# Sparse attention with a gated feed-forward: the softmax transposed by blocks on VectorE, the values product written straight into the columns of x

## The chip, the cores and the metric

The kernel runs on one core of one Trainium2 chip. The metric is the device time of one execution in microseconds (us), the median over runs; smaller is better. A core has TensorE (PE, matmuls, and beside it PEld, its weight loads), VectorE (DVE), ScalarE (ACT), GpSimd (POOL) and SyncE (SP), which issues the transfers here. Matmul results land in PSUM, eight banks of 128 partitions by 512 fp32 columns.

## The reference

Attention over 8 batches, 8 heads, 576 positions and 64 dimensions, then a feed-forward layer over its 4608 tokens (dm 512, dff 2048):

```python
scores = scale * np.matmul(q, k.transpose(0, 1, 3, 2))
mask_local = (rel >= 0) & (rel < 32)
mask_strided = (rel >= 0) & (pos[None, :] % 32 == pos[:, None] % 32)
...
attn = softmax(where(mask, scores, -1e9)) ; o = matmul(attn, v)
x = o.transpose(0, 2, 1, 3).reshape(B * S, H * D)
h = x @ w_in ; g = h * sigmoid(h) ; out = g @ w_out
```

Heads 0 to 3 use the local mask: a position sees itself and the 31 before it. Heads 4 to 7 use the strided one: a position sees the earlier ones with the same remainder by 32, at most 18. Everything is fp32.

## The kernel before, in words

**Tiles of the attention.** The host gathers q and k (`kqt`, dimensions on partitions, two heads on the 128 partitions) and v (`vt`) so that only the small blocks the masks leave are computed. A batch has six groups; the order in a batch is local, strided, local, strided, local, strided. A local group has 12 tiles of 32 queries by 64 keys for two heads, and a strided group 8, 8 or 6 tiles of 54 queries (3 remainders times 18) padded to 64 rows. Scores of a group stand in two PSUM banks (one for each head) as n column blocks of 128 rows: n is 3 for a local group (four tiles on top of one another in a block) and 4, 4 or 3 for the strided ones (two tiles in a block). `self.tiles` fixes which tile lies in which row block and column block, and so the order in which the matmuls are issued: before, tile t goes to column block `t // per` and row block `t % per`, so neighbouring tiles lie in different row blocks.

**Stages of a group** (methods of `Attention`). `scores` (L384) multiplies q and k, two matmuls a tile. `peak` (L402, and the exponential of ScalarE at L408) masks, takes the maximum and the exponential into `sm`, with the sums. `total` (L428, L429) makes reciprocals of the sums; `scale` (L432) multiplies `sm` by them, for strided groups alone. `turn` (L438) transposes `sm` on TensorE, one 128x128 matmul with the identity a column block, into a bank; `turned` (L442) copies that to `pt`. `values` multiplies by v: for a local group (L455) with rows of queries as the output, which `share` (L471) normalises into `xq` and `back` (L491) transposes on TensorE again, and `done` (L496) copies into `xb`; for a strided group (L460) with the head's dimensions as rows, which `sorted` (L484) copies into `xb` in the order of the positions. `xb` holds a batch's x, transposed, in fp32.

**Feed-forward.** The 4608 tokens are nine blocks of 512, and dff is 16 chunks of 128. For a block and chunk, `hidden` (L525) runs 12 matmuls of 128x128 by 128x512 over dm into one bank; `tanh` (L535, ScalarE), `gate` (L539), `ghi` (L547) and `glo` (L551, all VectorE) make the gated value and split it into a rounded part and a rest; `output` (L571) adds 12 more matmuls into four banks `po` that live through the block. fp32 precision comes from three products of rounded parts (hi by hi, hi by lo, lo by hi). At a block's end `store` copies each `po` on ScalarE into `osb` (L579), of which there are two, and sends it out. x is split into xhi and xlo at L513 and L517.

**Order.** PSUM is a ring `ps` of four banks, taken in turn by score halves, transposes, values and hidden chunks, and the four `po`. The first two batches, the loading of weights and block 0 are placed by a planner (`Steps`, `attention_steps`): each step has a cost on one or two engines and a due time, and it is put where it can start first; gaps on TensorE before 60 us are filled with transposes of the identity (L639). From block 1 on the order is written by hand: a chunk's `hidden`, its gating, and the `output` of the chunk before. At the chunks 0, 3, 5, 8, 11 and 13 of a block `between` inserts one **step** of the next batch's attention, behind the output:

```python
            c = plan[k, fc]
            turn(c + 1)
            back(c - 1)
            values(c)
            scores(c + 2)
            total(c + 2)
```

Of the kernel before, what the change touches and what calls it, by code (L numbers as in the profile page):

```python
# [28 lines left out]
P = 128  # L29
# [11 lines left out]


KW = 64
SEQ = 3 * NJ
QW = 448
VT = 12
KBUFS = 2
VBUFS = 2
KFIRST = 4
VFIRST = 6  # L50
XBUFS = NP + 2
# [6 lines left out]
class Group:  # L58
    def __init__(self, local, first, count):
        self.local, self.first, self.count = local, first, count  # L60
        self.rows = STRIDE if local else KW
        self.per = P // self.rows
        self.n = count // self.per
        step = STRIDE if local else SEQ
        self.q0 = [step * t for t in range(count)]
        half = S // STRIDE
        gap = [STRIDE if local and first < half <= first + t else 0 for t in range(count)]
        self.k0 = [q0 + g for q0, g in zip(self.q0, gap)]
        self.nq = self.q0[-1] + self.rows
        self.nk = self.k0[-1] + KW  # L70

        self.starts = [
            tuple(t % self.per for t in range(c * self.per, (c + 1) * self.per)
                  if local and (first + t) % half == 0)
            for c in range(self.n)
        ]
# [117 lines left out]
def sparse_attention_ffn(ctx: ExitStack, tc: tile.TileContext, kqt, vt, w_in, w_out, out):  # L194
# [55 lines left out]
    m = mask("mask_strided")  # L250
    for t in range(P // KW):
        keep(m, t * KW, KW, [4, NJ], [-NJ, -1], 0, 1)
        keep(m, t * KW, KW, [4, NJ], [NJ, 0], NJ - 1, -1)
    masks[False, ()] = m
# [98 lines left out]
    class Attention:  # L353


        def __init__(self, b, at):
# [83 lines left out]
        def turned(self, engine="ACT"):  # L440
            self.pt = att.tile([P, 512], F32, name="pt")
            copy[engine](out=self.pt[:, : self.cols], in_=self.psp[:, : self.cols])  # L442

        def values(self):
# [5 lines left out]
            for t, c, rows in self.tiles:  # L450
                p0 = c * P + rows.start
                for h in range(2):
                    at = slice(h * KW, (h + 1) * KW)
                    if g.local:
                        nc.tensor.matmul(  # L455
                            self.pso[h][rows, c * D : (c + 1) * D],
                            pt[at, p0 : p0 + g.rows], vbd[at, t], start=True, stop=True,
                        )
                    else:
                        nc.tensor.matmul(  # L460
                            self.pso[h * D : (h + 1) * D, t * SEQ : (t + 1) * SEQ], vbd[at, t],
                            pt[at, p0 : p0 + SEQ], start=True, stop=True,
                        )

        def share(self):
# [7 lines left out]
        def sorted(self):  # L473
            g, pso = self.g, self.pso

            places = STRIDE + 1
            at, end = 3 * g.first, 3 * (g.first + g.count)
            while at < end:
                hp, r = divmod(at, places)
                n = min(end - at, STRIDE - r)  # L480
                s0 = at - 3 * g.first
                src = pso[:, s0 * NJ : (s0 + n) * NJ].rearrange("p (r j) -> p r j", j=NJ)
# [10 lines left out]
        def done(self, engine="ACT"):  # L493
            flat = place_of(self.b).rearrange("p n s -> p (n s)")
            x0 = self.g.first * STRIDE
            copy[engine](out=flat[:, x0 : x0 + self.cols], in_=self.psx[:, : self.cols])  # L496

# [93 lines left out]
    def attention_steps(c, due, last=None):  # L591
# [16 lines left out]
        soft = e  # L608
        if not local:
            soft = add(f"N{c}", {"DVE": 0.14 + 0.14 * n}, t1 - 1, [r], a.scale)  # L610
        if last == "S":
# [4 lines left out]
                lambda: a.turned(p.engine), takes=["pt"], gives=[t])  # L616
        if last == "T":
            return
        v = add(f"v{c}", {"SP": P * a.g.count * D * 4 / RATE}, t2 - 5, [],
# [111 lines left out]
    nexts = [attention_steps(NG + i, burst[i : i + 4]) for i in range(NG)]  # L731
    attention_steps(2 * NG, (late[0], late[1], 0, 0), "T")
    attention_steps(2 * NG + 1, (late[1], late[1] + 8, 0, 0), "S")
# [24 lines left out]


    def scores(c):  # L760
        if c < len(groups):
# [11 lines left out]
    def turn(c):  # L773
        if c < len(groups):
            groups[c].turn()
            groups[c].turned()

    def values(c):
        if c < len(groups):
# [5 lines left out]
    def back(c):  # L785
        if groups[c].g.local:
            groups[c].back()
            groups[c].done()

# [99 lines left out]
```

## Time and profile before

| | us |
|---|---|
| median of 3 runs (920.74 to 921.81) | 921.0 |
| the profiled execution | 923.33 |
| its span | 921.5 |
| TensorE busy | 904.5 (98%) |
| VectorE busy | 436.6 (47%) |
| ScalarE busy | 315.1 (34%) |
| share of the chain that ended last: PE, DVE, DMA, ACT | 87%, 7%, 3%, 2% |

The span goes from the first to the last instruction of the profiled execution. The chain that ended last is followed back from the last instruction to what released each one. The largest groups are the matmuls of the hidden chunks (L525) and of the output (L571), 39% of that chain each.

### The profile page before, as it was taken

How to read it: one execution, taken by the hardware profiler on the slowest of the kernel's cores; microseconds unless marked ns; L12 is line 12 of the kernel's file. 1: busy time of each engine (PE TensorE's matmuls, PEld its weight loads, DVE VectorE, ACT ScalarE, POOL GpSimd, SP SyncE). 2: the span in 40 equal slices, each digit the busy share in tenths (PEclk: the TensorE clock that was granted, in tenths of full speed). 3: DMA queues.
4: the chain of work that ended last, by engine and by line, in shares of the span. 5: the costliest groups of instructions: out<-in, count | busy, mean ns of one | idle time of the engine just before them, and what ended most of it. 6: DMA issues, size and time to landing. Idle time of an engine off the chain costs nothing.

```text
span 921.5 us, 18028 instructions
## 1 busy us (share of the span) xinstructions
PE 904.5 (98%) x7451; PEld 742.9 (81%) x7451; DVE 436.6 (47%) x1408; ACT 315.1 (34%) x897; POOL 19.0 (2%) x38
## 2 busy tenths in 40 slices
PE   8999998999999999999999999999999999999997
PEld 6777776888888888888888888888888888888886
DVE  6999665434534444434444353444443333333332
ACT  3877453422532243224342252234332221112112
POOL 4100000000000000000000000000000000000000
PEclk9999999999999999999999999999999999999999
DMA  9674533201301102112220131120210010001001
GB/s 336 217 244 155 161 101 102 64 29 38 114 27 41 63 32 91 54 29 69 83 63 30 39 101 40 37 66 32 87 40 9 1 46 1 1 1 46 1 1 46
DMA packets 34962, 63.04 MB, mean 68 GB/s; under 512 B 2624, under 2 KB 22080, under 8 KB 34880
## 3 DMA queue, kind: packets, MB, share of 16 engines
q1 hardware_dynamic: 34880, 61.89, 20.3%
q8 instruction: 58, 0.95, 0.4%
q14 instruction: 24, 0.20, 0.1%
HBM read 52.45 MB, written 9.44 MB: 67 GB/s over the span
## 4 chain that ended last, share of the span: by engine, by line
PE 87%; DVE 7%; DMA 3%; ACT 2%; issue 0%; ACTq 0%; SPq 0%
PE ps L525 39%; PE po L571 39%; PE ps L384 3%; PE ps L460 2%; DMA stage<-w_in 2%; PE ps L438 1%; PE ps L455 1%; DVE stage L287 1%; DVE w L327 1%; DVE glo L551 1%; DVE sm L402 1%; PE ps L491 1%; DMA stage<-w_out 1%; DVE th L539 1%; PE ps L639 1%; ACT stage L276 1%
## 5 line engine op out<-in xcount | busy, mean ns | idle before, releaser
L525 PE MATMUL ps<-xhi,w 128*128 128x512 f32 x1152 | 386.6, 395 | 2.2 <-DVE th L539 1.5
L525 PEld LDWEIGHTS ps<-xhi,w 128*128 128x128 f32 x1152 | 216.2, 188 | 50.5 <-DVE th L539 1.9
L539 DVE SCALAR_TENSOR_TENSOR th<-th,ps 128x512 f32<-128x512 f32 (+1 forms) x147 | 99.3, 675 | 319.2 <-ACT th L535 319.1
L535 ACT ACTIVATE th<-ps 128x512 f32<-128x512 f32 (+1 forms) x147 | 86.3, 587 | 430.0 <-PE ps L525 427.7
L525 PE MATMUL ps<-xlo,w 128*128 128x512 f32 x576 | 225.2, 391 | 1.7 <-DVE xlo L517 1.7
L571 PE MATMUL po<-w,ghi 128*128 128x512 f32 x504 | 155.4, 390 | 0.7 <-ACT ghi L547 0.7
L525 PEld LDWEIGHTS ps<-xlo,w 128*128 128x128 f32 x576 | 108.2, 188 | 23.8 <-DVE xlo L517 3.0
L571 PEld LDWEIGHTS po<-w,ghi 128*128 128x128 f32 x504 | 94.4, 188 | 20.4 <-ACT ghi L547 0.8
L551 DVE TENSOR_TENSOR glo<-th,ghi 128x512 fp32r<-128x512 f32 (+1 forms) x147 | 100.3, 682 | 12.2 <-ACT ghi L547 1.6
L571 PE MATMUL po<-w,glo 128*128 128x512 f32 x252 | 98.3, 390 | 0.3 <-DVE glo L551 0.3
L571 PE MATMUL po<-stage,ghi 128*128 128x512 f32 x288 | 88.7, 389 | 0.0
L408 ACT ACTIVATE sm<-sm,sums 128x64 f32<-128x64 f32 x226 | 75.5, 336 | 13.2 <-DVE sums L402 12.6
L571 PE MATMUL po<-v,ghi 128*128 128x512 f32 x216 | 66.7, 390 | 0.0
L571 PEld LDWEIGHTS po<-stage,ghi 128*128 128x128 f32 x288 | 54.1, 188 | 11.3
L547 DVE CAST ghi<-th 128x512 fp32r<-128x512 f32 (+1 forms) x137 | 57.7, 421 | 10.4
L571 PEld LDWEIGHTS po<-w,glo 128*128 128x128 f32 x252 | 47.3, 188 | 11.0 <-DVE glo L551 1.2
L571 PE MATMUL po<-stage,glo 128*128 128x512 f32 x144 | 56.1, 389 | 0.0
L442 ACT COPY pt<-ps 128x384 f32<-128x384 f32 (+1 forms) x40 | 20.6, 514 | 79.8 <-PE ps L438 79.8
L571 PEld LDWEIGHTS po<-v,ghi 128*128 128x128 f32 x216 | 40.4, 188 | 8.5 <-ACT ghi L547 0.2
L571 PE MATMUL po<-k,ghi 128*128 128x512 f32 x144 | 44.3, 389 | 0.0
L571 PE MATMUL po<-v,glo 128*128 128x512 f32 x108 | 42.2, 391 | 0.4 <-DVE glo L551 0.4
L408 ACT ACTIVATION_READ_ACCUMULATOR sm<-sm,sums 128x1 f32 x226 | 42.6, 188 | 0.0
(77 smaller groups left out, 737.1 us busy)
## 6 DMA issues: line engine op xcount, KB each, us to landing
v<-vt SPq DMA_DIRECT2D x24, 384.0 KB, 3.6
out<-osb SPq DMA_DIRECT2D x36, 256.0 KB, 2.0
stage<-w_in SPq DMA_DIRECT2D x16, 512.0 KB, 4.8
stage<-w_out SPq DMA_DIRECT2D x16, 512.0 KB, 3.6
k<-kqt SPq DMA_DIRECT2D x16, 442.0 KB, 4.0
k<-kqt SPq DMA_DIRECT2D x16, 416.0 KB, 4.6
v<-vt SPq DMA_DIRECT2D x16, 256.0 KB, 2.8
k<-kqt SPq DMA_DIRECT2D x8, 448.0 KB, 4.2
```

Source lines behind the costliest of these rows:

```text
L276: nc.scalar.activation(out=value, in_=value, func=AF.Prelu, scale=2.0**-112, alpha=-(2.0**32))
L287: nc.vector.scalar_tensor_tensor(out=upper, in0=upper, scalar=3, in1=lower, op0=ALU.logical_shift_left, op1=ALU.bitwise_or,)
L384: nc.tensor.matmul(self.pss[h][rows, c * KW : (c + 1) * KW], kbd[at, 1, g.q0[t] : g.q0[t] + g.rows], kbd[at, 0, g.k0[t] : g.k0[t] + KW], s ...
L408: nc.scalar.activation(out=s_sb[:, c, h], in_=s_sb[:, c, h], func=AF.Exp, bias=peaks[:, c, h : h + 1], scale=-1.0, accum_out=rsum[:, c, h ...
L442: copy[engine](out=self.pt[:, : self.cols], in_=self.psp[:, : self.cols])
L460: nc.tensor.matmul(self.pso[h * D : (h + 1) * D, t * SEQ : (t + 1) * SEQ], vbd[at, t], pt[at, p0 : p0 + SEQ], start=True, stop=True,)
L525: nc.tensor.matmul(ph, weight(0, wi, fc)[:, cc * P : (cc + 1) * P], x[xi][cc], start=(cc, n) == (0, 0), stop=(cc, n) == (NP - 1, 2),)
L535: nc.scalar.activation(out=th[:, cols], in_=ph[:, cols], func=AF.Tanh, scale=0.5)
L539: nc.vector.scalar_tensor_tensor(out=th[:, cols], in0=th[:, cols], scalar=1.0, in1=ph[:, cols], op0=ALU.add, op1=ALU.mult,)
L547: copy[engine](out=g[0][:, cols], in_=th[:, cols])
L551: nc.vector.tensor_sub(out=g[1][:, cols], in0=th[:, cols], in1=g[0][:, cols].bitcast(F32))
L571: nc.tensor.matmul(po[tt], g[gi][:, cols], weight(1, wi, fc), start=fc == 0 and n == 0, stop=fc == NFC - 1 and n == 2,)
```

## The change

From the third batch on, all of the following. `scale` is applied to local groups as well. `turn_by_blocks` replaces `turn` and `turned`: VectorE transposes `sm` in blocks of 32x32 into `pt`, with two instructions over 128 partitions (each block stays on its own 32 partitions) and four over 32 partitions (the block goes to the neighbouring 32). `values_by_halves` replaces `values`, `share` and `back`: v is the stationary side for both kinds, the head's dimensions are the output's rows and the positions its columns; one half of a group's tiles reads the partitions 0 to 63, the other half 64 to 127, each half into a bank of its own, and `done_by_halves` copies them into `xb` on ScalarE. All of it but the values runs at the step that makes the scores, so `between` holds `values(c)` and `scores(c + 2)` alone.

For all batches, the first two included: `Group.at` numbers tiles down the column blocks of a row block first (tile t in column block `t % n`, row block `t // n`), so `self.tiles` issues all tiles of a row block before the next row block. Strided queries are padded to 64 in the host's layout (`QW` 448 to 512), and each group of 54 is cut in two halves of 27 at columns 0 and 32. Batches 0 and 1 keep the transposes on TensorE. In the planner the scale step is added for the group 2 * NG, and its transpose falls away: two `turn_by_blocks` stand ahead of block 1 instead.

```diff
+        self.at = [(t % self.n, t // self.n) for t in range(count)]
...
             self.tiles = [
-                (t, t // g.per, slice(t % g.per * g.rows, (t % g.per + 1) * g.rows))
-                for t in range(g.count)
+                (t, c, slice(r * g.rows, (r + 1) * g.rows)) for t, (c, r) in enumerate(g.at)
             ]
...
+        def turn_by_blocks(self):
+            n, size = self.g.n, P // STRIDE
+            pt = att.tile([P, 512], F32, name="pt")[:, : self.cols]
+            self.pt = pt = pt.rearrange("k (s c h q) -> k s c h q", s=2, h=2, q=STRIDE)
+            src = self.sm[:, : self.cols].rearrange("p (c h s k) -> p s c h k", h=2, s=2, k=STRIDE)
+            for s in range(2):
+                nc.vector.transpose(out=pt[:, s], in_=src[:, s])
+            for r in range(size):
+                rows, to = (slice(i * STRIDE, (i + 1) * STRIDE) for i in (r, r ^ 1))
+                nc.vector.transpose(out=pt[to, r % 2], in_=src[rows, 1 - r % 2])
...
+        def values_by_halves(self):
+            g, pt, vbd = self.g, self.pt, self.vbd
+            self.pso = [self.bank("pso") for _ in range(2)]
+            half, size = g.count // 2, STRIDE if g.local else SEQ
+            for i in range(half):
+                for p in range(2):
+                    c, r = g.at[p * half + i]
+                    at = slice(p * KW, (p + 1) * KW)
+                    for h in range(2):
+                        moved = pt[at, r % 2, c, h] if g.local else pt[at, :, c, h, :HALF]
+                        nc.tensor.matmul(
+                            self.pso[p][h * D : (h + 1) * D, i * size : (i + 1) * size],
+                            vbd[at, 2 * i + h], moved, start=True, stop=True,
+                        )
+
+        def done_by_halves(self):
+            g = self.g
+            half = g.count // 2
+            if g.local:
+                flat = place_of(self.b).rearrange("p n s -> p (n s)")
+                for p in range(2):
+                    x0, n = (g.first + p * half) * STRIDE, half * STRIDE
+                    nc.scalar.copy(out=flat[:, x0 : x0 + n], in_=self.pso[p][:, :n])
+                return
+            for p in range(2):
+                first = g.first + p * half
+                self.sort(self.pso[p], 3 * first, 3 * (first + half))
...
     def scores(c):
         if c < len(groups):
             groups[c].scores()
             scored.add(c)
             load_due()
             groups[c].peak()
-
-    def total(c):
-        if c < len(groups):
             groups[c].total()
-            if not groups[c].g.local:
-                groups[c].scale()
...
+            groups[c].scale()
+            groups[c].turn_by_blocks()
 
     def values(c):
-        if c < len(groups):
-            groups[c].values()
-            weighed.add(c)
-            load_due()
-            (groups[c].share if groups[c].g.local else groups[c].sorted)()
...
+        groups[c].values_by_halves()
+        weighed.add(c)
+        load_due()
+        groups[c].done_by_halves()
...
         if (k, fc) in plan:
-            c = plan[k, fc]
-            turn(c + 1)
-            back(c - 1)
-            values(c)
-            scores(c + 2)
-            total(c + 2)
-
+            values(plan[k, fc])
+            scores(plan[k, fc] + 2)
+
+    for c in (2 * NG, 2 * NG + 1):
+        groups[c].turn_by_blocks()
```

Line numbers shift: in the changed kernel the scores are at L389, the exponential at L413, the values at L495, hidden at L580, tanh at L590, gate at L594, ghi at L602, glo at L606, output at L626, the idle transposes at L692.

TensorE's order at a block's first step (a local group; `stage` names hold w_out), before:

```order
L571 MATMUL po<-stage_1734,ghi 128x512
L571 MATMUL po<-stage_1730,glo 128x512
L438 MATMUL ps<-ident,sm 128x128 x4
L455 MATMUL ps<-v_77,pt 32x64 x24
L384 MATMUL ps<-k_80 32x64 x24
L525 MATMUL ps<-xhi,w_0_616 128x512
```

and of the changed kernel:

```order
L626 MATMUL po<-stage_1769,ghi 128x512
L626 MATMUL po<-stage_1767,glo 128x512
L495 MATMUL ps<-pt,v_77 64x32 x24
L389 MATMUL ps<-k_80 32x64 x24
L580 MATMUL ps<-xhi,w_0_598 128x512
```

The four transposes of the next group are gone; 24 values and 24 scores stand between the output and the hidden chunk as before, the values with 32 moving columns instead of 64 and 64 output rows instead of 32.

TensorE at the second step (a strided group), before:

```order
L571 MATMUL po<-w_0_701,glo 128x512
L438 MATMUL ps<-ident,sm 128x128 x3
L491 MATMUL ps<-ident,xq 128x128 x3
L460 MATMUL ps<-pt,v_77 64x54 x16
L384 MATMUL ps<-k_81 64x64 x16
L525 MATMUL ps<-xhi,w_0_616 128x512
```

and now:

```order
L626 MATMUL po<-w_0_709,glo 128x512
L495 MATMUL ps<-pt,v_77 64x54 x16
L389 MATMUL ps<-k_81 64x64 x16
L580 MATMUL ps<-xhi,w_0_598 128x512
L580 MATMUL ps<-xlo,w_0_598 128x512
```

Both sets of transposes are gone, the next group's softmax and the result of the local group before.

VectorE behind the scores of a strided group with n = 4, before:

```order
L428 TENSOR_SCALAR sums<-sums 128x8
L429 RECIPROCAL sums<-sums 128x8
L432 TENSOR_TENSOR sm<-sm,sums 128x512
L539 SCALAR_TENSOR_TENSOR th<-th,ps 128x512
L547 CAST ghi<-th 128x512
L551 TENSOR_TENSOR glo<-th,ghi 128x512
```

and now:

```order
L433 TENSOR_SCALAR sums<-sums 128x8
L434 RECIPROCAL sums<-sums 128x8
L437 TENSOR_TENSOR sm<-sm,sums 128x512
L594 SCALAR_TENSOR_TENSOR th<-th,ps 128x512
L459 STREAM_TRANSPOSE pt<-sm 128x256 x2
L602 CAST ghi<-th 128x512
L462 STREAM_TRANSPOSE pt<-sm 32x256 x4
L606 TENSOR_TENSOR glo<-th,ghi 128x512
```

The six block transposes stand between the gate and glo of the hidden chunk of that step.

## Rows read from the trace of the kernel before

**Rows 1.** Windows by stage: us, busy by engine, PEclk, DMA, GB/s.

```profile
0.00:113.00 113.00, 104.63 (x1294) 82.94 (x1294) 93.41 (x321) 70.14 (x125) 17.04 (x36) 0.98 0.67 222
148.40:728.30 579.90, 579.90 (x5010) 479.93 (x5007) 252.29 (x892) 195.92 (x682) 0.00 (x0) 1.00 0.16 52
```

**Rows 2.** Timeline of PE at a local step: start, us, line, tiles, count.

```profile
446.38 0.60 PE L438 MATMUL ps<-ident,sm 128*128 128x128 f32 x4
446.91 0.72 PE L455 MATMUL ps<-v,pt 64*32 64x64 f32 x48
447.43 0.93 PE L384 MATMUL ps<-k 64*32 64x64 f32 x48
448.29 0.50 PE L525 MATMUL ps<-xhi,w 128*128 128x512 f32 x1
```

**Rows 3.** Timeline of PE at the next step, a strided one.

```profile
464.74 0.49 PE L438 MATMUL ps<-ident,sm 128*128 128x128 f32 x3
...
465.49 1.07 PE L460 MATMUL ps<-pt,v 64*64 64x54 f32 x29
466.35 0.27 PE L384 MATMUL ps<-k 64*64 64x64 f32 x1
466.35 0.22 PE L460 MATMUL ps<-pt,v 64*64 64x54 f32 x1
...
466.40 0.23 PE L460 MATMUL ps<-pt,v 64*64 64x54 f32 x2
...
467.03 0.50 PE L525 MATMUL ps<-xhi,w 128*128 128x512 f32 x1
```

**Rows 4.** Timeline of PE, last step of the same batch, first and last row.

```profile
527.81 0.49 PE L438 MATMUL ps<-ident,sm 128*128 128x128 f32 x3
...
529.87 0.50 PE L525 MATMUL ps<-xhi,w 128*128 128x512 f32 x1
```

**Rows 5.** Timeline of PE in the first 40 us: strided scores, local scores.

```profile
13.02 0.69 PE L384 MATMUL ps<-k 64*64 64x64 f32 x32
13.64 0.72 PE L455 MATMUL po<-v,pt 64*32 64x64 f32 x48
...
28.15 0.72 PE L384 MATMUL ps<-k 64*32 64x64 f32 x48
28.80 0.44 PE L639 MATMUL ps<-ident 128*128 128x128 f32 x2
```

**Rows 6.** Timeline of ACT at two block starts, 444 and 743 us.

```profile
444.53 1.28 ACT L579 ACTIVATE osb<-po 128x512 f32<-128x512 f32 x2
...
742.95 1.28 ACT L579 ACTIVATE osb<-po 128x512 f32<-128x512 f32 x2
745.67 1.29 ACT L579 ACTIVATE osb<-po 128x512 f32<-128x512 f32 x2 [1.45 <-DMA out<-osb]
```

**Rows 7.** Lines by form: line, tiles, count, busy us, mean ns, idle before.

```profile
L547 DVE CAST ghi<-th 128x512 fp32r<-128x512 f32 x133 | 56.8, 427 | 10.3
L484 ACT COPY xb<-ps 128x144 f32<-128x144 f32 x7 | 2.9, 408 | 2.3 <-PE ps L460 2.3
L517 DVE TENSOR_TENSOR xlo<-xb,xhi 128x256 fp32r<-128x256 f32 x8 | 3.1, 422 | 4.2 <-ACT xhi L513 4.2
L517 DVE TENSOR_TENSOR xlo<-xb,xhi 128x192 fp32r<-128x192 f32 x8 | 2.8, 354 | 4.0 <-ACT xhi L513 4.0
```

**Rows 8.** Timeline of DVE at a step with n = 4.

```profile
533.51 0.69 DVE L432 TENSOR_TENSOR sm<-sm,sums 128x512 f32<-128x512 f32 x1
534.12 0.68 DVE L539 SCALAR_TENSOR_TENSOR th<-th,ps 128x512 f32<-128x512 f32 x1
```

**Rows 9.** Critical chain in order of time: start, us, what.

```profile
443.81 2.72 PE po L571 x12
...
448.36 2.94 PE ps L525 x12
```

**Rows 10.** Timeline of PE where block 1 begins.

```profile
146.44 0.63 PE L438 MATMUL ps<-ident,sm 128*128 128x128 f32 x4 [1.84 <-DVE sm L432]
```

More of the change, by code (lines that the diff above doesn't have):

```diff
@@ L49 @@
 KFIRST = 4
+EARLY = 2
 VFIRST = 6
@@ L63, in __init__ @@
         self.n = count // self.per
-        step = STRIDE if local else SEQ
-        self.q0 = [step * t for t in range(count)]
+        self.q0 = [self.rows * t for t in range(count)]
         half = S // STRIDE
         gap = [STRIDE if local and first < half <= first + t else 0 for t in range(count)]
-        self.k0 = [q0 + g for q0, g in zip(self.q0, gap)]
+        self.k0 = [(STRIDE if local else SEQ) * t + g for t, g in enumerate(gap)]
         self.nq = self.q0[-1] + self.rows
         self.nk = self.k0[-1] + KW
+        self.at = [(t % self.n, t // self.n) for t in range(count)]
         self.starts = [
-            tuple(t % self.per for t in range(c * self.per, (c + 1) * self.per)
-                  if local and (first + t) % half == 0)
+            tuple(r for t, (at, r) in enumerate(self.at)
+                  if at == c and local and (first + t) % half == 0)
             for c in range(self.n)
@@ L250, in sparse_attention_ffn @@
     m = mask("mask_strided")
-    for t in range(P // KW):
-        keep(m, t * KW, KW, [4, NJ], [-NJ, -1], 0, 1)
-        keep(m, t * KW, KW, [4, NJ], [NJ, 0], NJ - 1, -1)
+    for t in range(P // STRIDE):
+        q0 = t % 2 * HALF
+        keep(m, t * STRIDE, STRIDE, [4, NJ], [-NJ, -1], q0, 1)
+        keep(m, t * STRIDE, STRIDE, [4, NJ], [NJ, 0], NJ - 1 - q0, -1)
     masks[False, ()] = m
@@ L440, in turned @@
         def turned(self, engine="ACT"):
-            self.pt = att.tile([P, 512], F32, name="pt")
-            copy[engine](out=self.pt[:, : self.cols], in_=self.psp[:, : self.cols])
+            pt = att.tile([P, 512], F32, name="pt")
+            copy[engine](out=pt[:, : self.cols], in_=self.psp[:, : self.cols])
+            self.pt = pt[:, : self.cols].rearrange("k (c r q) -> k c r q", r=P // STRIDE, q=STRIDE)
+        def turn_by_blocks(self):
[8 more added lines that the diff above has]
+                nc.vector.transpose(out=pt[to, r % 2], in_=src[rows, 1 - r % 2])
         def values(self):
@@ L450, in values @@
             for t, c, rows in self.tiles:
-                p0 = c * P + rows.start
+                r = rows.start // STRIDE
                 for h in range(2):
@@ L456, in values @@
                             self.pso[h][rows, c * D : (c + 1) * D],
-                            pt[at, p0 : p0 + g.rows], vbd[at, t], start=True, stop=True,
+                            pt[at, c, r], vbd[at, t], start=True, stop=True,
                         )
@@ L473, in sorted, with sort @@
         def sorted(self):
-            g, pso = self.g, self.pso
+            g = self.g
+            self.sort(self.pso, 3 * g.first, 3 * (g.first + g.count))
+        def sort(self, pso, first, end):
             places = STRIDE + 1
-            at, end = 3 * g.first, 3 * (g.first + g.count)
+            at = first
             while at < end:
@@ L495, in done @@
             x0 = self.g.first * STRIDE
[L496 removed]
+            dst = flat[:, x0 : x0 + self.cols].rearrange(
+                "p (r c q) -> p c r q", c=self.g.n, q=STRIDE
+            )
+            src = self.psx[:, : self.cols].rearrange("p (c r q) -> p c r q", c=self.g.n, q=STRIDE)
+            copy[engine](out=dst, in_=src)
     def new_x():
@@ L608, in attention_steps @@
         soft = e
-        if not local:
+        if not local or a.b >= EARLY:
             soft = add(f"N{c}", {"DVE": 0.14 + 0.14 * n}, t1 - 1, [r], a.scale)
@@ L865, in rows @@
         flat = np.concatenate([flat, np.zeros((B, 2, 1, D), a.dtype)], axis=2)
-        tiles = flat[:, :, where].transpose(0, 2, 1, 4, 3, 5)
-        return np.ascontiguousarray(tiles).reshape(B, NG, P, VT, D)
+        tiles = flat[:, :, where]
+        by_head = tiles[:EARLY].transpose(0, 2, 1, 4, 3, 5).reshape(EARLY, NG, P, VT, D)
+        by_tile = np.zeros((B - EARLY, NG, 2, KW, VT // 2, 2, D), a.dtype)
+        for gi, g in enumerate(GROUPS):
+            half = g.count // 2
+            some = tiles[EARLY:, :, gi, : g.count].reshape(B - EARLY, 2, 2, half, KW, D)
+            by_tile[:, gi, :, :, :half] = some.transpose(0, 2, 4, 3, 1, 5)
+        return np.concatenate([by_head, by_tile.reshape(B - EARLY, NG, P, VT, D)])
     kq = np.ascontiguousarray(np.stack([columns(k, k_from), columns(q, q_from)], axis=3))
```

22 lines of the change are left out of this document (7 added, 15 removed).

## The prediction

> **What bounds the kernel now.** Read the stages first [rows 1]. Up to 113 us TensorE is busy 104.6 us, with VectorE at 93.4 of 113 beside it; from 148.4 to 728.3 us TensorE is busy for every microsecond while VectorE is at 252 of 580 and ScalarE at 196. So from 148 us on only TensorE's own instructions, or a new wait on it, move the end. This stage holds the attention of the batches 2 to 7, which is what the change rewrites. Next, TensorE by itself in such a stretch, at a local step [rows 2] and at a strided step [rows 3]. A step is all that stands between an output and the next hidden chunk: 446.38 to 448.29 (1.91 us) and 464.74 to 467.03 (2.29 us). Read in the same way, the six steps of a batch take 1.91, 2.29, 1.91, 2.17, 1.70 and 2.06 us, in all 12.04; the last of them is in [rows 4].
>
> Three prices come from these rows. A 128 by 128 transpose costs 0.11 us: six of them and the change to small tiles behind them take 464.74 to 465.49, 0.75 us, so 0.10 is the change of shape. A matmul with 64 rows is two passes (x32 for 16 matmuls). The strided values use two tiles of the array in turn: from 465.49 to 466.40 each does 15 passes after its first, 0.06 us a pass. The strided scores on four tiles take 13.02 to 13.64, that is 0.62 with a change of shape at the end [rows 5], for 8 passes a tile: again 0.06 a pass, whatever runs beside it. So a stage costs **passes per tile times 0.06**, and what counts is how many tiles work at once. The change of shape behind small tiles is 0.13: 28.15 to 28.80 with it against 446.91 to 447.43 without [rows 2, 5].
>
> **The change part by part.** The sum is for one batch in the TensorE-bound stage.
>
> *Removed.* 20 transposes of the softmax and 9 of the result, 29 x 0.11 = -3.2 us. The 0.10 for the first change of shape stays, now between the output and the values. ScalarE's copies of pt and VectorE's normalisation leave engines that have room.
>
> *Values.* Four tiles are now used in turn. Strided with 16 matmuls: 32 passes on four tiles, 8 each, 0.48 us, against 0.92 [rows 3]; with 12 matmuls 0.36. Local: 48 passes on four tiles are 12 each, 0.72 us, and 0.13 since the scores behind it have another shape; it was 0.52 on eight tiles [rows 2]. The moving side shrinks from 64 to 32 columns, but the pass was 0.06 with 54 and with 64, so I take no gain from that.
>
> *Scores.* Nothing in scores is edited, yet its order changes: the tiles now run down one row block before the next, so neighbouring matmuls want the same two tiles. What this costs depends on how far TensorE lets a later matmul pass one that waits. At 466.35 a score matmul starts on a free tile while the last values still have a pass to come at 466.40, and though the first score in program order must wait for a tile that they hold [rows 3]. It does so just when the last values begin, not earlier. I read it so: each tile takes one running matmul and one waiting, and dispatch blocks behind a third. Then row block r+1 starts when r has two matmuls left. Local: three starts 0.12 apart and 6 passes, 0.72 us (+0.13 shape); strided with n=4: 0.24 + 0.48 = 0.72 (+0.13), with n=3 0.12 + 0.36 = 0.48 (+0.13).
>
> Steps after: local 0.10 + 0.85 + 0.87 = 1.82, three times; strided 0.10 + 0.48 + 0.85 = 1.43, then 0.10 + 0.48 + 0.61 = 1.19, then 0.10 + 0.36 + 0.85 = 1.31. In all 9.39 for 12.04, **-2.65 us a batch**. (This also drops the 0.2 us that scores wait today for the bank of psp.)
>
> *New waits on a bank.* The ring has four banks, so the next hidden chunk takes the bank of the first half of the values, and waits for ScalarE's copy out of it. (a) At a block's first step ScalarE has four osb copies queued ahead. Today pt's copy stands between them; without attention the third starts 2.72 us after the first and the fourth ends 4.0 after it, since each waits for the store of an earlier osb [rows 6]. From 444.53 that is 448.54, then some 0.3 for the copy (0.41 is the nearest row, for 144 columns in a strided order [rows 7]): the bank is free at 448.9, TensorE wants it 1.82 us after 446.38, at 448.2. +0.7 us in five blocks. (b) The fourth step's first half is copied in two pieces, 0.41 for 144 columns and some 0.25 for 54, begun 0.3 after the values' end, against scores of 0.61: 0.3 us late. Elsewhere the scores cover it. So 6 x (-2.65 + 0.3) + 5 x 0.7 = **-10.6 us**.
>
> *Added on VectorE:* a scale for the local groups and six block transposes a group, two over 128 and four over 32 partitions, 192 or 256 elements each. No row shows one. Bounds: a cast of 128x512 takes 0.43, so at its rate 0.2; the longest plain pass of VectorE, 128x512, 0.69. I take the row with the same elements, a plain fp32 tensor_tensor: 0.35 and 0.42 [rows 7]. They hide only if glo stays in time, because the queue has gate, two transposes, ghi, four transposes, glo. At the heaviest step (n=4, hidden starting 529.87) the scale ends at 534.1 and the gate at 534.8 [rows 8]; then 0.84, 0.46, 1.68 and 0.69 put glo at 538.5. TensorE wants it two matmuls (0.45) into the output that starts 2.94 + 2 x 2.72 after 529.87 [rows 4, 9], at 538.7. It fits by 0.2 us; n=3 fits by 1.3. With 0.69 apiece glo is 1.5 us late at n=4 and 0.8 at n=3: 11 x 1.5 + 23 x 0.8 = +35 us; with 0.2, nothing is gained, as TensorE doesn't wait there. A rule beside it: the Trainium skill, "VectorE: DVE Perf Modes", section on two Vector instructions with no wait between them, says that one whose input or output begins in another quadrant of 32 partitions starts only after all earlier ones have finished. The small transposes change quadrant each time. Rows overlap neighbours by some 0.08 us (533.51, 0.69 long; the next at 534.12); by the rule six transposes lose 0.5, glo is 0.3 late at n=4, and the sum is +3 us more. No run here shows it.
>
> *First two batches.* They keep transposes and copies but get the new order: scores +0.2 for each of 7 local groups and +0.1 to 0.24 for 7 strided, local values +0.2 for six: some 4 us of TensorE work in a stage where it has 8 us of gaps in 113 [rows 1], and the strided k loads grow from 442 to 512 columns. Bounds 0 (all in gaps) and +6 (all on the path, with half as much again for the replanned order); I take the middle, +3. *Change-over:* VectorE now also has to turn two groups before block 1's first values, while TensorE already stands 1.84 us for its scale [rows 10]: six transposes at 0.35 for what was a wait on the scale, less the turn and copy on the way, +1 (0 to +2).
>
> **Sum:** -10.6 + 3 + 1 = -6.6. Against the profiled execution (923.33 us with a span of 921.5) that is 916.7; the median of the runs is 921.0, 2.3 lower, so I give **914.4 us**. About 0.2%, 1.8 us, is what a measurement of this kernel can tell from no change.
>
> **The rivals.**
> *Scores keep their speed* (any free tile starts at once): then scores stay near today's 0.65 and 0.62, some 0.2 a group less than above in 34 groups: 908 us. Against it: the early start at 466.35 came only with the last values. The change then does just what it says.
> *VectorE late:* if a transpose of 256 costs over 0.45 us, or one of 192 over 0.56, glo comes after TensorE wants it. At 0.6 and 0.5 it is 0.9 late in 11 groups: +10, **925 us**. For it: the slack is 0.2 us and six instructions share the error; against it: VectorE is at 44%, and n=3 has 1.3.
> *Scores in strict order:* no matmul passes a waiting one. Then local scores are 24 passes, 1.44, and strided 0.96 and 0.72: +0.7 and +0.24 a group, +16 us in the long stage and some +3 in the first two batches: **933 us**. The Trainium skill, "TensorE: Matmul & The Clock Gate", Part 3, says that matmuls start and end strictly in program order. The trace disagrees at 466.35, where a score starts ahead of a pass of the values.
> *The front is hit harder:* its chain takes all of the extra work and the replanned order is worse: 921 us, no change.
>
> **How the numbers follow.** Forecast 0.55 (its own range 908 to 920 from the bounds of front and change-over and 0.1 a step either way), scores at full speed 0.13, VectorE late 0.17, strict order 0.07, front 0.08. Faster by over 0.2%: 0.52 + 0.13 = 0.65. Within 0.2%: 0.03 + 0.05 = 0.08 (the forecast's upper end and the front). Slower: 0.17 + 0.07 + 0.03 = 0.27. The range leaves out strict order and the far ends: 905 to 927.
>
> **What would show it.** Right: local steps near 1.8 us with scores of 0.7 to 0.9, strided steps of 1.2 to 1.45, no transposes after 150 us, the hidden chunk waiting some 0.7 us for a copy at each block's start. Wrong: output matmuls waiting for glo or ghi (VectorE late), scores of 1.4 us (strict), or the first block's end later by more than 4 us.

## The result and the profile after

The changed kernel takes 911.45 us (median of 4 runs, 910.58 to 913.12) against 921.4 us (920.74 to 922.92) beside it: ratio 0.9892, 95% interval 0.9872 to 0.9912, some 10.0 us faster. The forecast was 914.4 with a range of 905 to 927. Its profiled execution is 913.12 us with a span of 911.3, so both the executions and the spans differ by 10.2.

The page's first lines, and two windows (us, busy and count of PE, PEld, DVE, ACT, POOL, then PEclk, DMA share, GB/s), answer to [rows 1]:

```profile
span 911.3 us, 17917 instructions
PE 893.3 (98%) x7297; PEld 731.9 (80%) x7297; DVE 505.6 (55%) x1604; ACT 302.1 (33%) x899; POOL 19.8 (2%) x42
```

```profile
0.00:113.00 113.00, 105.18 (x1304) 85.95 (x1304) 91.73 (x319) 71.21 (x127) 17.77 (x40) 1.00 0.68 226
147.70:718.90 571.20, 566.85 (x4847) 463.94 (x4844) 321.38 (x1087) 182.90 (x683) 0.00 (x0) 1.00 0.18 55
```

The long stage is still TensorE's: it is idle for 4.4 us of 571 now, where it was never idle before. VectorE went from 252 to 321 us there. The timeline of PE (start, us, line, tiles, count) at the second step answers to [rows 3], at the third, a local one, to [rows 2]; the last two rows are the scores of the fourth:

```profile
460.41 0.69 PE L495 MATMUL ps<-pt,v 64*64 64x54 f32 x32
460.92 0.94 PE L389 MATMUL ps<-k 64*64 64x64 f32 x32
461.79 0.50 PE L580 MATMUL ps<-xhi,w 128*128 128x512 f32 x1
...
472.92 0.90 PE L495 MATMUL ps<-pt,v 64*64 64x32 f32 x48
473.75 0.97 PE L389 MATMUL ps<-k 64*32 64x64 f32 x48
474.65 0.50 PE L580 MATMUL ps<-xhi,w 128*128 128x512 f32 x1
...
491.72 0.71 PE L389 MATMUL ps<-k 64*64 64x64 f32 x24
492.48 0.50 PE L580 MATMUL ps<-xhi,w 128*128 128x512 f32 x1
```

From one start to the next: local values 0.83 and scores 0.90, strided values 0.51 and scores 0.87, with the shape's change in it. With the 0.1 ahead of them a step takes 1.82 (local), and 1.47, 1.36 and, in the same view, 1.35 (the three strided ones). At a block's start it takes 2.52, and what it waits for stands in the PE row, in the waits of the long stage, and on ACT:

```profile
441.42 0.90 PE L495 MATMUL ps<-pt,v 64*64 64x32 f32 x48
442.25 0.97 PE L389 MATMUL ps<-k 64*32 64x64 f32 x48
443.85 0.50 PE L580 MATMUL ps<-xhi,w 128*128 128x512 f32 x1 [0.63 <-ACT xb L507]
```

```profile
PE ps L580 <- ACT xb L507: 3.1, 5, 0.6
```

```profile
442.20 0.60 ACT L634 ACTIVATE osb<-po 128x512 f32<-128x512 f32 x1 [1.44 <-DMA out<-osb]
442.99 0.60 ACT L634 ACTIVATE osb<-po 128x512 f32<-128x512 f32 x1 [0.19 <-DMA out<-osb]
443.48 0.54 ACT L507 COPY xb<-ps 128x192 f32<-128x192 f32 x2
```

The third osb copy waits 1.44 us for a store, the copy of the values stands behind the fourth, and the hidden chunk behind that: five times, 3.1 us.

VectorE at a step with n = 4 (the place of [rows 8]), and its transposes in the lines by form (count, busy, mean ns):

```profile
466.01 0.68 DVE L594 SCALAR_TENSOR_TENSOR th<-th,ps 128x512 f32<-128x512 f32 x1
466.61 0.77 DVE L459 STREAM_TRANSPOSE pt<-sm 128x256 f32<-128x256 f32 x2
467.29 0.39 DVE L602 CAST ghi<-th 128x512 fp32r<-128x512 f32 x1
467.71 1.79 DVE L462 STREAM_TRANSPOSE pt<-sm 32x256 f32<-32x256 f32 x4
469.53 0.69 DVE L606 TENSOR_TENSOR glo<-th,ghi 128x512 fp32r<-128x512 f32 x1
```

```profile
L462 DVE STREAM_TRANSPOSE pt<-sm 32x192 f32<-32x192 f32 x96 | 35.5, 370 | 1.8
L462 DVE STREAM_TRANSPOSE pt<-sm 32x256 f32<-32x256 f32 x48 | 21.0, 436 | 0.9
L459 DVE STREAM_TRANSPOSE pt<-sm 128x192 f32<-128x192 f32 x48 | 15.2, 354 | 0.1
L459 DVE STREAM_TRANSPOSE pt<-sm 128x256 f32<-128x256 f32 x24 | 9.2, 421 | 0.0
```

glo ends at 470.22, and TensorE wants it at 470.56 (the third output matmul): it fits by 0.34 us. At the change-over to block 1, the place of [rows 10], the PE timeline now shows

```profile
145.14 0.30 PE L495 MATMUL ps<-pt,v 64*64 64x32 f32 x4 [0.34 <-DVE pt L462]
145.63 1.25 PE L495 MATMUL ps<-pt,v 64*64 64x32 f32 x44 [0.19 <-DVE pt L462]
...
157.50 0.50 PE L626 MATMUL po<-w,glo 128*128 128x512 f32 x1 [0.88 <-DVE glo L606]
```

Two times divide the span, both starts of a hidden chunk in the PE timeline: behind the second step of block 1, and behind the last values. Before, they are 167.17 and 728.33; now 166.85 and 718.12. Between them lie 34 steps: 561.16 before, 551.27 now, so **9.9 of the 10.2 us come from these 34 steps**, and 0.3 from all ahead of them. The profiles that follow repeat the stretch to 0.1 us where nothing in it is edited. The part ahead of it scatters: seven of the kernels below, the changed one among them, have the same first two batches, and in their traces the output behind block 1's first hidden chunk starts between 138.67 and 144.50 us (141.92 in the changed kernel's). So the 0.3 is not resolved.

### The profile page after: what moved, and what is told of

It is laid out like the page before. It is cut to its first block, busy times and chain, and to the rows that moved or that the text cites. A ratio compares the mean times of both kernels' runs of the same rounds, so it can differ in the third digit from the quotient of the medians.

```text
span 911.3 us, 17917 instructions
## 1 busy us (share of the span) xinstructions
PE 893.3 (98%) x7297; PEld 731.9 (80%) x7297; DVE 505.6 (55%) x1604; ACT 302.1 (33%) x899; POOL 19.8 (2%) x42
## 4 chain that ended last, share of the span: by engine, by line
PE 86%; DVE 7%; DMA 4%; ACT 2%; issue 1%; ACTq 0%; DVEq 0%; SPq 0%
PE ps L580 40%; PE po L626 39%; PE ps L389 3%; PE ps L495 2%; DMA out<-osb 1%; DVE stage L293 1%; DMA stage<-w_out 1%; DVE w L333 1%; DMA stage<-w_in 1%; DVE sm L407 1%; DVE th L594 1%; DVE glo L606 1%; ACT osb L634 1%; DVE xlo L572 1%; DVE pt L462 1%
## 5 line engine op out<-in xcount | busy, mean ns | idle before, releaser
L580 PE MATMUL ps<-xhi,w 128*128 128x512 f32 x1152 | 386.2, 395 | 5.7 <-ACT xb L507 3.1
L580 PEld LDWEIGHTS ps<-xhi,w 128*128 128x128 f32 x1152 | 216.0, 188 | 54.9 <-ACT xb L507 3.9
L594 DVE SCALAR_TENSOR_TENSOR th<-th,ps 128x512 f32<-128x512 f32 (+1 forms) x147 | 99.2, 675 | 237.1 <-ACT th L590 236.9
L590 ACT ACTIVATE th<-ps 128x512 f32<-128x512 f32 (+1 forms) x147 | 86.4, 588 | 426.1 <-PE ps L580 423.7
L580 PE MATMUL ps<-xlo,w 128*128 128x512 f32 x576 | 224.4, 390 | 0.0
L626 PE MATMUL po<-w,ghi 128*128 128x512 f32 x504 | 155.5, 390 | 0.0
L580 PEld LDWEIGHTS ps<-xlo,w 128*128 128x128 f32 x576 | 108.2, 188 | 21.2
L626 PEld LDWEIGHTS po<-w,ghi 128*128 128x128 f32 x504 | 94.4, 188 | 19.7
L606 DVE TENSOR_TENSOR glo<-th,ghi 128x512 fp32r<-128x512 f32 (+1 forms) x147 | 100.0, 681 | 10.6
L626 PE MATMUL po<-w,glo 128*128 128x512 f32 x252 | 98.2, 390 | 0.9 <-DVE glo L606 0.9
L626 PE MATMUL po<-stage,ghi 128*128 128x512 f32 x288 | 88.9, 390 | 0.0
L413 ACT ACTIVATE sm<-sm,sums 128x64 f32<-128x64 f32 x226 | 75.6, 336 | 14.2 <-DVE sums L407 13.5
L626 PE MATMUL po<-v,ghi 128*128 128x512 f32 x216 | 66.6, 390 | 0.0
L602 DVE CAST ghi<-th 128x512 fp32r<-128x512 f32 (+1 forms) x142 | 58.6, 413 | 9.2
L626 PEld LDWEIGHTS po<-stage,ghi 128*128 128x128 f32 x288 | 53.9, 188 | 11.2
L462 DVE STREAM_TRANSPOSE pt<-sm 32x192 f32<-32x192 f32 (+1 forms) x144 | 56.5, 392 | 2.7
L626 PEld LDWEIGHTS po<-w,glo 128*128 128x128 f32 x252 | 47.3, 188 | 11.2 <-DVE glo L606 1.3
L626 PE MATMUL po<-stage,glo 128*128 128x512 f32 x144 | 56.0, 389 | 0.0
L626 PEld LDWEIGHTS po<-v,ghi 128*128 128x128 f32 x216 | 40.5, 188 | 8.4
L389 PE MATMUL ps<-k 64*32 64x64 f32 (+1 forms) x1856 | 45.7, 226 | 1.3 <-DMA k<-kqt 0.7
L626 PE MATMUL po<-k,ghi 128*128 128x512 f32 x144 | 44.3, 389 | 0.0
L389 PEld LDWEIGHTS ps<-k 64*32 64x32 f32 (+1 forms) x1856 | 39.2, 120 | 5.5 <-issue 3.0
```

Source lines behind the costliest of these rows:

```text
L389: nc.tensor.matmul(self.pss[h][rows, c * KW : (c + 1) * KW], kbd[at, 1, g.q0[t] : g.q0[t] + g.rows], kbd[at, 0, g.k0[t] : g.k0[t] + KW], s ...
L413: nc.scalar.activation(out=s_sb[:, c, h], in_=s_sb[:, c, h], func=AF.Exp, bias=peaks[:, c, h : h + 1], scale=-1.0, accum_out=rsum[:, c, h ...
L462: nc.vector.transpose(out=pt[to, r % 2], in_=src[rows, 1 - r % 2])
L580: nc.tensor.matmul(ph, weight(0, wi, fc)[:, cc * P : (cc + 1) * P], x[xi][cc], start=(cc, n) == (0, 0), stop=(cc, n) == (NP - 1, 2),)
L590: nc.scalar.activation(out=th[:, cols], in_=ph[:, cols], func=AF.Tanh, scale=0.5)
L594: nc.vector.scalar_tensor_tensor(out=th[:, cols], in0=th[:, cols], scalar=1.0, in1=ph[:, cols], op0=ALU.add, op1=ALU.mult,)
```

## The experiments

Each run is told by its ratio to the kernel before on the same chip (the changed kernel: 0.9892) and, from its trace, by the stretch of 34 steps. A kernel with one execution is read by its trace alone.

| run | median us | ratio, 95% interval | 34 steps, us |
|---|---|---|---|
| before | 921.4 | | 561.16 |
| changed | 911.45 | 0.9892 (0.9872 to 0.9912) | 551.27 |
| scores_across_rows | 908.24 | 0.9848 (0.9831 to 0.9864) | 547.14 |
| first_half_copied_by_vector | 909.17 | 0.9860 (0.9845 to 0.9875) | 548.23 |
| scores_and_copy | 905.42 | 0.9814 (0.9794 to 0.9834) | 543.84 |
| scores_and_copy_front | 905.51 | 0.9811 (0.9790 to 0.9832) | 543.74 |
| scores_tile_by_tile | 927.92, one run | | 563.99 |
| values_half_by_half | 920.2, one run | | 559.20 |
| small_transposes_twice | 926.27, one run | | 556.09 |
| before_turn_behind | 921.32, one run | | 561.16 |
| before_wide_loads | 923.89 | 1.0015 (1.0000 to 1.0029) | 561.21 |
| front_rows_first | 912.95 | 0.9902 (0.9885 to 0.9919) | 551.19 |

### The order of the scores

```diff
-            for t, c, rows in self.tiles:
+            for t, c, rows in sorted(self.tiles, key=lambda x: (x[1], x[2].start)):
```

(in `scores`, from the third batch on)

> From the third batch on the score matmuls are issued down the row blocks first again, as in the kernel before (next row block before next column block); all else as in the changed kernel. Theory (each tile of the array takes one running and one waiting matmul, and issue blocks behind a third, so the changed order starts row blocks 0.12 us apart): local scores fall from 0.90 to some 0.65 us, which shows in 13 of 18 local steps as -0.2 (at five block starts the wait for ScalarE's copy takes it). Strided scores could fall from 0.87 to 0.62, but then the bank of the first half of the values is still being copied by ScalarE: from the rows at 461 us (copy from 461.13, some 0.57 us, next hidden chunk at 461.79) -0.1 at the second step, 0 at the fourth and -0.2 at the sixth. Sum 2.6 + 1.8 = -4.4 us against the changed kernel, about 907. Rival 1 (only the passes of each tile count, not their order): no change, 911.4. Rival 2 (order is all and copies hide): 18 x 0.22 + 12 x 0.25 + 6 x 0.13 = -7.7, about 904.

Measured: 4.1 us less in the 34 steps. The local scores, 0.90 us in the changed kernel, are

```profile
370.85 0.72 PE L392 MATMUL ps<-k 64*32 64x64 f32 x48
371.50 0.50 PE L583 MATMUL ps<-xhi,w 128*128 128x512 f32 x1
```

0.65 again. The waits of the long stage show where the rest stayed: the bank of the first half is released later than the shorter scores need it.

```profile
PE ps L583 <- ACT xb L510: 4.4, 5, 0.9
PE ps L583 <- ACT xb L538: 1.3, 6, 0.2
```

So the order alone costs the changed kernel 4 us: rival 1 falls, and so does rival 2, whose -7.7 had the copies hidden. The other way round, with the scores of one tile all in a row:

```diff
+            pairs = [(h, *x) for x in self.tiles for h in range(2)]
+            pairs.sort(key=lambda x: (x[0], x[3].start, x[2]))
-            for t, c, rows in self.tiles:
-                for h in range(2):
+            for h, t, c, rows in pairs:
```

> From the third batch on the scores are issued tile by tile of the array: all matmuls of one head and row block, then the next. Theory (one running and one waiting on each tile, issue blocks behind a third): with three matmuls a tile the next tile starts 0.12 us later, so local scores take 7 x 0.12 + 0.36 = 1.20 and 0.13 for the shape; strided ones with four matmuls a tile 3 x 0.24 + 0.48 = 1.20, with three 3 x 0.12 + 0.36 = 0.72. Against 0.72, 0.72 and 0.48 of the changed kernel: 18 x 0.48 + 12 x 0.48 + 6 x 0.2, less 5 x 0.48 that the wait at block starts swallows: +13 us, about 924. Rival 1 (strict order, no matmul starts ahead of one that waits): the next tile starts with the last matmul of the one before, local 8 x 0.24 + 0.12 = 2.04, strided 4 x 0.36 + 0.12 = 1.56, +35 us or more, 946. Rival 2 (order does not matter, only passes of a tile): 911.4.

Measured: 12.7 us more in the 34 steps (theory 13, strict order 35). Local scores, start to start, take 1.44 where the theory said 1.33 and strict order 2.17, strided ones 1.43 where it said 1.33:

```profile
382.36 1.51 PE L392 MATMUL ps<-k 64*32 64x64 f32 x48
383.80 0.50 PE L583 MATMUL ps<-xhi,w 128*128 128x512 f32 x1
```

### The values on two tiles at a time

```diff
-            for i in range(half):
-                for p in range(2):
+            for p in range(2):
+                for i in range(half):
```

> The values are issued one half after the other, so two tiles of the array work in turn at a time, as the strided values did in the kernel before. Theory (one running and one waiting matmul a tile): the second half starts when the first has two matmuls a tile left: local 0.48 + 0.72 = 1.20 for 0.72, strided 0.24 + 0.48 = 0.72 for 0.48 and with 12 matmuls 0.12 + 0.36 = 0.48 for 0.36. At block starts the wait for the copy takes it all. 13 x 0.48 + 6 x 0.24 + 6 x 0.07 (step 4 waits for a copy today) + 6 x 0.12 = +8.8 us in the long stage, local steps 2.3. Rival 1 (the halves do not overlap at all): local 1.44, strided 0.96 and 0.72, +17 us. Rival 2 (only the passes in all count): no change.

Measured: 7.9 us more. Local values take 1.32 instead of 0.83, that is +0.49 for the 0.48 worked out. The 0.9 missing from 8.8 lie at the block starts, which the theory left as they were: ScalarE's order there now has the copy ahead of the fourth osb, and the step takes 2.31 instead of 2.52, five times.

```profile
376.45 1.39 PE L495 MATMUL ps<-pt,v 64*64 64x32 f32 x48
377.77 0.97 PE L389 MATMUL ps<-k 64*32 64x64 f32 x48
```

Both rivals fall: with neighbours on two tiles instead of four, values in the new layout leave 2.0 of the 9.9 us (559.20 against 561.16 before). (It is no measure of the transposes' share, since the local values took 0.52 us on eight tiles before [rows 2].)

### The wait at a block's start

```diff
-                    nc.scalar.copy(out=flat[:, x0 : x0 + n], in_=self.pso[p][:, :n])
+                    copy[("DVE", "ACT")[p]](out=flat[:, x0 : x0 + n], in_=self.pso[p][:, :n])
```

(the same for the pieces of the strided groups)

> VectorE instead of ScalarE copies the first half of the values out of its bank, everything else as in the changed kernel. Theory (the hidden chunk at a block's start waits for that copy, which stands behind four osb copies on ScalarE): the wait of 0.7 us goes at five block starts, -3.5 us, and the fourth step loses some 0.1 in each batch, -0.6; about 907.5. VectorE is idle when the values end, and the peaks behind the copy wait for the scores anyway, so nothing is added there. Rival 1 (the wait at a block's start is something else, such as the scores or the new po banks): 911.4. Rival 2 (VectorE's queue has only 0.3 us left at a step with n = 4 and the copy of 0.3 to 0.45 goes on top): -3.5 + 11 x 0.1 and more, 909 to 912, with the output's matmuls waiting for glo.

Measured: 3.0 us less. The wait for ScalarE is gone from the view of waits, and at a block's start the hidden chunk follows the scores, a step of 1.82:

```profile
439.79 0.97 PE L389 MATMUL ps<-k 64*32 64x64 f32 x48
440.69 0.50 PE L580 MATMUL ps<-xhi,w 128*128 128x512 f32 x1
```

That is the theory's 3.5; the 0.6 of the fourth step did not come: it takes 1.45 instead of 1.36, with the hidden chunk 0.14 us behind VectorE's two copies (they end at 391.61, it starts at 391.75), where it was 0.05 behind ScalarE's. Both edits together:

> The two edits together: scores down the row blocks first from the third batch on, and the first half of the values copied by VectorE. From the steps measured singly: local steps 1.58, also at a block's start where either edit alone leaves 2.52 or 1.82, so 5 x 0.94 = 4.7 there; the other local steps 13 x 0.24 = 3.1; strided steps 1.40, 1.45 and 1.2 (VectorE's copy of 216 columns takes 0.53, as ScalarE's does, so the bank still bounds them) for 1.47, 1.36 and 1.35: -0.8. Theory (two causes that add up, and more at block starts): -8.6 us against the changed kernel, ratio to the kernel before near 0.980. Rival (block starts are held by something behind the copy, so the gains overlap): -4.1 - 3.0 and no more, 0.9815 or above.

Measured: 7.4 us less, ratio 0.9814: faster than both kernels, as its twin below is. The steps say the theory (1.58 at each block's start), the sum lies nearer to the rival's 7.1. Of the 1.2 us missing from 8.6, 0.5 is the theory's count: it took 13 other local steps at 0.24, and the 34 steps hold 11 with scores; all steps together fell by 8.1. The other 0.7 came back between the steps: 0.8 where block 2 begins and 0.3 and 0.2 at the blocks 3 and 4, less 0.6 in the other chunks. At block 2 VectorE's order has the six transposes ahead of the gate (its timeline, then PE's):

```profile
248.85 0.64 DVE L462 STREAM_TRANSPOSE pt<-sm 128x192 f32<-128x192 f32 x2
249.52 1.52 DVE L465 STREAM_TRANSPOSE pt<-sm 32x192 f32<-32x192 f32 x4
251.07 0.69 DVE L597 SCALAR_TENSOR_TENSOR th<-th,ps 128x512 f32<-128x512 f32 x1
251.79 0.43 DVE L605 CAST ghi<-th 128x512 fp32r<-128x512 f32 x1
```

```profile
252.27 0.73 PE L629 MATMUL po<-w,ghi 128*128 128x512 f32 x2 [0.20 <-DVE ghi L605]
253.00 0.50 PE L629 MATMUL po<-w,glo 128*128 128x512 f32 x1
```

### VectorE's room

```diff
+                for _ in range(2):
                     nc.vector.transpose(out=pt[to, r % 2], in_=src[rows, 1 - r % 2])
```

> Each of the four transposes over 32 partitions is done twice. Theory (they stand ahead of glo on VectorE; at a step with n = 4 glo ends 470.22 and TensorE wants it at 470.56, so 0.34 us are left, with n = 3 about 1.3): 4 x 0.45 = 1.8 more makes glo 1.45 late in 11 groups, and 4 x 0.39 = 1.56 more makes it 0.26 late in 23: 16 + 6 = +22 us, about 933, and TensorE's output matmuls wait for glo. Rival (VectorE is busy for 55% of the span, so there is room): no change, 911.4.

A miss by its mechanism. The 34 steps grew by 4.8 us, not 22: in 31 of the last 35 groups the compiled order of VectorE still has four of the eight ahead of glo, and the other four behind it. Seven stretches between two steps grew by 0.4 to 1.0 us each, which together is all of the 4.8. In five of them the four behind glo, with pieces of the next block's xlo among them, stand ahead of the next chunk's gate and ghi; in two, all eight stand ahead of a gate. TensorE's weight loads for the output wait there for ghi (3.7 us) and for glo (3.0 us). What grew besides is the change-over, which the expectation left out: step 2 ends 8.3 us later. Two waits on PE, and the window around them:

```profile
147.59 2.06 PE L496 MATMUL ps<-pt,v 64*64 64x32 f32 x48 [3.26 <-DVE pt L463]
163.57 0.74 PE L627 MATMUL po<-w,ghi 128*128 128x512 f32 x2 [2.67 <-DVE ghi L603]
```

```profile
143.00:170.00 27.00, 21.00 (x158) 16.45 (x157) 20.34 (x59) 6.66 (x21) 0.66 (x1) 0.81 0.21 70
```

There VectorE turns three groups close together and is on the path; the granted clock of this window is 0.81 on average. It fell during the wait of 3.26 us: from 147.59 to 151.00 us it is 0.50, the lower of its two levels of 1.2 and 2.4 GHz, and there 48 local values take 2.06 us for 0.90.

### The change-over

The kernel before, with block 1's first step alone in another order:

```diff
-            turn(c + 1)
+            if c > 2 * NG:
+                turn(c + 1)
             back(c - 1)
             values(c)
             scores(c + 2)
             total(c + 2)
+            if c == 2 * NG:
+                turn(c + 1)
```

> The kernel before, with one edit: at block 1's first step the transposes of the next group's softmax stand behind the values and the scores instead of ahead of them. Theory (the 2.6 us that the changed kernel gains at the change-over come from this, that TensorE's queue no longer holds the next group's transposes ahead of the present group's values): the wait of 1.84 us shrinks by the 1.3 that values and scores take, the step of 3.94 us (144.44 to 148.38) to about 2.7, the time by 1.3. Rival (VectorE's load sets the change-over, so the wait moves to the values or the hidden chunk behind): the step stays at 3.9.

Measured: the step takes 2.77 for 3.94 us, 1.2 less, and nothing behind it moves (the 34 steps are 561.16 both times):

```profile
144.29 0.71 PE L384 MATMUL ps<-k 64*32 64x64 f32 x48
146.07 0.63 PE L438 MATMUL ps<-ident,sm 128*128 128x128 f32 x4 [1.06 <-DVE sums L402]
146.45 0.47 PE L525 MATMUL ps<-xhi,w 128*128 128x512 f32 x1
```

So TensorE stood in front of the present group's values for the next group's softmax. The expectation's 2.6 us, though, are not one gain. They are read between the starts of two hidden chunks (137.26 to 148.38 before, 139.20 to 147.71 now), and the first of these chunks is not the same length in both. PE from its first matmul to the output behind it, before:

```profile
137.26 0.50 PE L525 MATMUL ps<-xhi,w 128*128 128x512 f32 x1 [0.46 <-DVE th L539]
137.93 0.50 PE L525 MATMUL ps<-xlo,w 128*128 128x512 f32 x1 [0.17 <-DVE xlo L517]
140.44 0.50 PE L525 MATMUL ps<-xlo,w 128*128 128x512 f32 x1 [0.83 <-DVE xlo L517]
141.72 0.62 PE L571 MATMUL po<-stage,ghi 128*128 128x512 f32 x2
```

and of the changed kernel, without a wait:

```profile
139.20 0.39 PE L580 MATMUL ps<-xhi,w 128*128 128x512 f32 x1
141.92 0.61 PE L626 MATMUL po<-stage,ghi 128*128 128x512 f32 x2
```

Before, the chunk begins early, waits for VectorE and takes 4.46 us; now it takes 2.72. So 1.7 of the 2.6 us lie inside this chunk, and 0.9 in the change-over behind it (6.66 us from that output's start to the next hidden chunk before, 5.79 now).

### The front

In `scores` and `values`, for the first two batches alone (in the first of the two runs for all batches, with both edits above):

```diff
+        def down(self):
+            early = self.b < EARLY
+            return sorted(self.tiles, key=lambda x: (x[1], x[2].start)) if early else self.tiles
...
-            for t, c, rows in self.tiles:
+            for t, c, rows in self.down():
```

> As the kernel before it in this list, and the first two batches too issue their scores and values down the row blocks first. Theory (the +2.0 us that the changed kernel has at 138 us come from the order of these matmuls: 0.25 us a local value or score group and 0.1 to 0.25 a strided one, in a stage where TensorE has gaps): 2 us less than the kernel before it. Rival (the front is set by loads and ScalarE's and VectorE's work on the weights, and the 2 us are a scatter of the planner's fills and of the loads): no difference between the two.

> The changed kernel with scores and values of the first two batches alone issued down the row blocks first again. Theory of the order: 2 us less than the changed kernel, ratio 0.987 to before. Rival (loads and plan): as the changed kernel, 0.989.

And the kernel before with the wider loads:

```diff
-QW = 448
+QW = 512
...
-        self.nq = self.q0[-1] + self.rows
+        self.nq = self.q0[-1] + self.rows if local else self.rows * count
```

> The kernel before with the strided loads of q and k widened to the 512 (384 for the third) columns of the changed kernel, which also moves the planner's placement in block 0; the matmuls and their order inside a group stay. Theory (the +2.0 us that the changed kernel has at 138 us come from the wider loads and the plan that follows from them): 2 us slower than before, ratio 1.002, with the marks of block 0 later by 1 to 2 us. Rival (they come from the order of the matmuls inside a group): no change, ratio 1.000.

Restoring the order in the first two batches shows no gain: 0.9811 beside 0.9814, and 0.9902 beside 0.9892, where the theory's 0.987 lies outside the interval. The wider loads, with the plan that follows from them, cost 0.15% with an interval from 0 to 0.29%, which holds the theory's 1.002 and no change alike. The order is not worth 2 us, then, and the rows of the change-over say that there may be nothing to find: the 2 us are the later start of a chunk that no longer waits, and at its end 0.2 us of them are left (141.92 for 141.72). Nor do the other traces show a later front: the seven with the changed one have that mark at 141.2 us on average, scattered over 5.8, and the two with the front of before at 141.72 and 140.96. A cost or gain of the front below that scatter stays open.

## Why the prediction was right, and where it was off

**The sum over steps held.** It gave local 1.82 and strided 1.43, 1.49 (1.19 with 0.3 late) and 1.31; measured are 1.82, 1.47, 1.36 and 1.35. For the 34 steps the text's terms are 6 x (-2.65 + 0.3) + 5 x 0.7 = -10.6, less -0.95 for the first two steps: -9.65 for a measured -9.89 (the steps themselves fell by 10.3, and 0.4 came back in the chunks between them). Its three prices (0.06 a pass on each tile, 0.11 a transpose, 0.13 for the shape) came from the kernel before. No run takes the transposes away by themselves, so their share, 29 x 0.11 a batch, rests on these rows and on the steps adding up.

**The order of the scores** was the term that the diff does not show in `scores`. The reading of it, one running and one waiting matmul a tile, gave the right size in three orders: 4.1 us for 4.4, +12.7 for +13, +7.9 for +8.8. It is a model that these lengths bear out, not something seen; tile by tile it was 0.1 short, and whether the place that fills up is the matmul's or its weight load's no run separates. "Scores keep their speed" and "strict order" fall with it. The Trainium skill, "TensorE: Matmul & The Clock Gate", Part 3, has matmuls start strictly in program order; by that the tile by tile run would have grown by 35 us and not by 12.7, and in values_half_by_half a score starts at 364.25 us while six passes of the values ahead of it have still to start.

**The wait at a block's start** was forecast as 0.7 us in five blocks, and is that: 2.52 for 1.82, gone when VectorE copies.

**VectorE's bounds held for the wrong reason.** A transpose was taken as 0.35 and 0.42 and is 0.354 and 0.421 over 128 partitions, 0.370 and 0.436 over 32. The margin at n = 4 is 0.34 for a forecast 0.2. The rival "VectorE late" priced further delay as if the queue were fixed; the doubled transposes show that the compiled order moves. The same backlog did appear, once, at the change-over: 0.88 us for glo at 157.50. The trace agrees with the rule of the Trainium skill ("VectorE: DVE Perf Modes", two Vector instructions with no wait between them): four small transposes take 1.79 us for 4 x 0.436, no overlap, while the two over 128 partitions take 0.77 for 2 x 0.421. The 0.5 us that the prediction added by it did not come, because its sum had counted every transpose at full length already.

**The term that was mis-sized is the front's "+3".** The prediction took the middle between 0 (all in gaps) and +6 (all on the path). Up to the output behind block 1's first hidden chunk TensorE is busy for 131.74 us before and 134.10 now, and that output starts 0.2 us later (141.72, 141.92): in these two executions the added 2.4 us of work went into gaps, which is the lower bound. The scatter over executions, 5.8 us, is larger than the term.

**The change-over, "+1 (0 to +2)", came out near +0.4, in part by luck.** From that output's start to the end of step 2 the time fell by 0.52 us (25.45 to 24.93), where the forecast's first two steps alone give -0.95. The prediction counted VectorE's six transposes, but two things that it did not have nearly cancel. The 1.84 us of [rows 10] were a wait for the *next* group's scale, which TensorE no longer needs ahead of the present group's values: the next hidden chunk starts 0.9 us earlier against the output. And glo's delay at 157.50 gives 1.2 back.

Front 2.8, change-over 0.6 and the steps 0.2 make up the 3.6 us between the forecast's -6.6 and the profile's -10.2.

## What to carry to other kernels

Price small matmuls by passes per tile of the array and by how many tiles take turns, and look at the order in which a renumbering makes neighbours share a tile: here it took back 4 of 14 us without a line of the stage being edited. Moving work off a full engine is worth more where its in-order queue held that work ahead of something already ready, so ask of each wait whose data it is for. Read a stage's length between marks that lie behind its last wait: here a mark at the start of a chunk that waits inside itself showed a loss of 1.9 us ahead of it and a gain of 1.7 behind it, and 0.2 was left at the chunk's end. A shortened step hands the end to the next bank that must be copied out: look who copies it and what stands ahead in that engine's queue.

## What the runs showed of the hardware

A VectorE block transpose costs by its columns, hardly by its partitions: 128x256 0.421 us, 32x256 0.436. VectorE and ScalarE take the same time, 0.53 us, to copy 128x216 from a bank into strided places (534 and 532 ns by form), so moving that copy gains only the queue. And a wait of 3.26 us on TensorE, in which its granted clock fell from 1.00 to 0.50, was followed by matmuls at over twice their time (2.06 us for 0.90).
